# Making a 64-token tail as a 128-row chunk, and joining two batches' k-v products in one run, in an attention + bilinear FFN kernel on TensorE

## The chip, the cores and the metric

The kernel runs on one core of one Trainium2 chip. The metric is the device time of one execution in microseconds (us); the lower the better. A profile names the engines PE (TensorE matmuls), PEld (TensorE weight loads), DVE (VectorE), ACT (ScalarE), POOL (GpSimd) and SP (SyncE, whose queue issues many of the DMAs). In the code, `P` is the kernel's tile in PSUM, where its matmuls write; the second index of `P` is what is called a bank here. L258 is line 258 of the kernel that the profile belongs to, so a line that moved has another number after an edit: the attention chunk is L258 before and L265 after, the kv product is L168 in both.

## The reference, cut to what matters

```python
B, H, S, D = 8, 8, 576, 64           # batches, heads, tokens, head size
kv  = einsum('bhsd,bhse->bhde', k, v)        # per head 64 x 64
out = einsum('bhsd,bhde->bhse', q, kv)
x   = out / sqrt(mean(out**2, -1) + 1e-6) * g_norm    # per token and head
x   = x as (4608 tokens, 512)
y   = ((x @ w_a) * (x @ w_b)) @ w_out        # 512 -> 1536 -> 512
```

The last product chain is nearly all of the arithmetic. A batch has 576 tokens, which is four and a half times 128: each batch ends in a half chunk of 64 tokens.

## The kernel before

The FFN runs over nine strips of 512 tokens. A strip is 12 units `ffn_ab` (eight matmuls of 512 columns each) and 4 units `ffn_o` (twelve each). Strips 1 to 6 hold, between these dense units, the attention of the batch that the next strip needs: batch 2 in strip 1, and so on to batch 7 in strip 6. `slot(A, s, n)` is called after each unit with whole `n`, and in the middle of each with `n - 0.5`.

```python
# the product of k and v of one batch: 4 head pairs x 5 token chunks x 2 heads = 40 matmuls.
# Each has 64 weight columns; the two heads of a pair write rows 0 to 63 and rows 64 to 127 of o.
def kv(self, p, o):
    ...
    for c, n in enumerate(rows):
        for j in range(2):
            nc.tensor.matmul(o[j * D : (j + 1) * D, :],
                             lhsT=kk[0:n, 2 * p + j, c, :], rhs=vv[0:n, 2 * p + j, c, :], ...)

# one chunk of tokens of the batch: 4 matmuls, weights = q (tokens as columns)
def tx(self, c, i):
    t0 = c * 128
    n = min(128, S - t0)                    # the fifth chunk has n = 64
    for p in range(NP):
        nc.tensor.matmul(P[0:n, i, p * 128 : (p + 1) * 128],
                         lhsT=self.qT[:, p, t0 : t0 + n],
                         rhs=kvb[self.b % 2][:, p, :], start=True, stop=True)
    nc.scalar.activation(sqt[c % 3][0:n], P[0:n, i, :]..., AF.Square)
# then tss (DVE: sum), trs (ACT: 1/sqrt, POOL: times g), txt (DVE: product, SP: transpose to xt)

def slot(A, s, n):
    kb = P[:, 7, 0 : NP * D]...             # PSUM bank 7
    k0, xs = (5, (6.5, 8, 9.5, 11, 12.5)) if s == 1 else (2, (3.5, 5, 6, 7.5, 8.5))
    if n == k0:
        for p in range(NP):
            A.kv(p, kb[:, p, :])
        A.kv_out(slice(0, NP), kb)          # ACT copies kv to SBUF
    for c, x in enumerate(xs):
        i = 5 + c % 3                       # PSUM banks 5, 6, 7
        if n == x:         A.tx(c, i)
        elif n == x + 0.5: A.tss(c)
        elif n == x + 1:   A.trs(c)
        elif n == x + 2.5: A.txt(c, i)
# per strip: transpose q of batch b+1 at n = 8 (12 in strip 1), load batch b+2 at n = 14
```

## Time and profile before

The kernel takes 317.67 us (median of 3 runs, 317.66 to 318.12). Its profiled execution spans 316.0 us.

| before | value | view |
|---|---|---|
| PE busy | 309.6 us, 98% | engine table |
| DVE, ACT, POOL busy | 44%, 37%, 32% | engine table |
| chain that ended last, on PE | 95% | chain |
| PE's own waits | 2.9 us, all before 62 us | waits |
| a dense 512-column matmul, start to start | 215 to 217 ns | start times in the trace |

The engine table of before, and the chain of work that ended last, as shares of the span by engine and by line:

```profile
PE 309.6 (98%) x1907; PEld 147.0 (47%) x1907; DVE 138.5 (44%) x230; ACT 115.9 (37%) x229; POOL 101.7 (32%) x124
...
PE 95%; DMA 4%; issue 0%; POOL 0%; ACT 0%; POOLq 0%
PE P L312 59%; PE P L369 30%; PE P L258 2%; DMA qt<-in_q_dram 2%; DMA vt<-in_v_dram 2%; PE P L168 2%; PE P L219 0%; PE P L192 0%; PE P L245 0%; PE P L206 0%; ACT o_end L595 0%; POOL ident masks.py:199 0%; POOL ident masks.py:197 0%; POOLq masks.py:199 0%; POOLq L611 0%
```

The kernel is bound by PE. But "98% busy" does not say what PE loses: the record of a 512-column matmul lasts 379 ns while the next starts 216 ns later, so records overlap and paper over short pauses. What has to be read is the step from one start to the next. The waits of the weight loads give a first hint. Columns: who waited, for what, us in total, times, longest:

```profile
PEld L168 <- issue: 3.8, 10, 0.4
PEld L258 <- issue: 2.5, 6, 0.4
```

L258 runs 30 chunks, but only six of them show such a pause of 0.4 us: one a batch. Here are PE's instructions in order of time around a full chunk, around the last chunk of batch 5, and around its kv run. Columns: start in us, length, engine, line, operation, weight shape, matrix streamed, how many:

```profile
160.99 1.03 PE L312 MATMUL P<-xt,wb_t 128*128 128x512 bf16 x4
161.86 0.39 PE L258 MATMUL P<-kvb,qT 128*128 128x128 bf16 x4
162.08 1.03 PE L312 MATMUL P<-xt,wa_t 128*128 128x512 bf16 x4
...
167.71 1.03 PE L312 MATMUL P<-xt,wa_t 128*128 128x512 bf16 x4
168.66 0.41 PE L258 MATMUL P<-kvb,qT 128*64 128x128 bf16 x4
169.01 1.04 PE L312 MATMUL P<-xt,wb_t 128*128 128x512 bf16 x4
...
154.73 1.03 PE L312 MATMUL P<-xt,wb_t 128*128 128x512 bf16 x4
155.69 0.82 PE L168 MATMUL P<-vtl,ktl 128*64 128x64 bf16 x40
156.44 1.04 PE L312 MATMUL P<-xt,wa_t 128*128 128x512 bf16 x4
```

Four dense matmuls take 4 x 216 = 864 ns. So the full chunk adds 162.08 - 160.99 - 0.864 = 0.23 us, and the last chunk, with half the rows, adds 169.01 - 167.71 - 0.864 = 0.44 us. From the start times of single instructions (last dense start before to second dense start after, less two steps of 216) it is 224 ns against 447 ns, and 858 ns for a kv run. All figures of "what a piece adds" below are made in this way. The weight loads of the last chunk show where the pause sits:

```profile
167.71 0.53 PEld L312 LDWEIGHTS <-wa_t 128*128 128x128 bf16 x3
168.66 0.25 PEld L258 LDWEIGHTS <-qT 128*64 128x64 bf16 x4 [0.42 <-issue]
169.00 0.33 PEld L312 LDWEIGHTS <-wb_t 128*128 128x128 bf16 x3
```

The last dense matmul started at 168.354, and at the usual step of 216 ns the next matmul would have started at 168.57, but the next load of weights came only at 168.66, 308 ns after that start and 2 ns ahead of its own matmul. The first load of the full chunk at 161.86 us comes 214 ns ahead of its matmul, 3 ns after the start of the dense matmul before it.

### The profile page before, as it was taken

What the parts mean: (1) busy time and instruction counts of PE and PEld (TensorE: products, weight loads), DVE (VectorE), ACT (ScalarE), POOL (GpSimd) and SP (SyncE); (2) the same over time, 40 slices, a digit from 0 to 9 for tenths busy, and PEclk for the clock granted to TensorE, in tenths of its full rate; (3) what the DMA queues carried; (4) which work ended last, traced back from release to release, by engine and by line L of the source; (5) the groups of instructions that cost most, each with busy time, mean ns of one, the idle gap of its engine ahead of it and who ended that gap; (6) DMA issues with size and microseconds to landing.
All of it is one profiled execution on the core that took longest, in us unless ns stands there. A gap on an engine that the chain in (4) does not pass through costs nothing.

```text
span 316.0 us, 4979 instructions
## 1 busy us (share of the span) xinstructions
PE 309.6 (98%) x1907; PEld 147.0 (47%) x1907; DVE 138.5 (44%) x230; ACT 115.9 (37%) x229; POOL 101.7 (32%) x124
## 2 busy tenths in 40 slices
PE   7899999999999999999999999999999999999995
PEld 3444464444454444544454445444544444444443
DVE  4544335356337603771267224832475134213321
ACT  3643155453246214630455025512561232123310
POOL 8954890192543640346024801410041000000000
PEclk9999999999999999999999999999999999999999
DMA  8999999999999699069906992463012200030002
GB/s 177 197 196 199 200 183 156 228 126 172 173 172 136 119 173 184 17 127 133 227 10 125 133 229 21 81 104 100 2 35 72 105 0 0 33 97 5 0 35 100
DMA packets 94237, 36.19 MB, mean 115 GB/s; under 512 B 64902, under 2 KB 89734, under 8 KB 94214
## 3 DMA queue, kind: packets, MB, share of 16 engines
q0 software_dynamic: 59120, 18.44, 54.1%
q1 hardware_dynamic: 34738, 17.01, 23.8%
q10 hardware_dynamic: 356, 0.43, 0.4%
q8 instruction: 15, 0.25, 0.3%
q14 instruction: 8, 0.07, 0.1%
HBM read 37.78 MB, written 12.98 MB: 161 GB/s over the span
## 4 chain that ended last, share of the span: by engine, by line
PE 95%; DMA 4%; issue 0%; POOL 0%; ACT 0%; POOLq 0%
PE P L312 59%; PE P L369 30%; PE P L258 2%; DMA qt<-in_q_dram 2%; DMA vt<-in_v_dram 2%; PE P L168 2%; PE P L219 0%; PE P L192 0%; PE P L245 0%; PE P L206 0%; ACT o_end L595 0%; POOL ident masks.py:199 0%; POOL ident masks.py:197 0%; POOLq masks.py:199 0%; POOLq L611 0%
## 5 line engine op out<-in xcount | busy, mean ns | idle before, releaser
L330 DVE TENSOR_TENSOR ab<-P,asb 128x512 bf16<-128x512 f32 x108 | 74.5, 691 | 109.1 <-PE P L312 91.2
L312 PE MATMUL P<-xt,wa_t 128*128 128x512 bf16 x432 | 111.9, 379 | 0.0
L312 PE MATMUL P<-xt,wb_t 128*128 128x512 bf16 x432 | 111.8, 379 | 0.0
L326 ACT CAST asb<-P 128x512 bf16<-128x512 f32 x108 | 63.0, 585 | 90.9 <-PE P L312 90.9
L369 PE MATMUL P<-wo_t,ab 128*128 128x512 bf16 (+1 forms) x444 | 95.8, 374 | 0.0
L369 PEld LDWEIGHTS <-ab 128*128 128x128 bf16 x444 | 43.0, 98 | 48.7
L312 PEld LDWEIGHTS <-wb_t 128*128 128x128 bf16 x432 | 41.3, 98 | 47.7 <-DMA wb_t<-in_moe_w_b_dram 0.6
L312 PEld LDWEIGHTS <-wa_t 128*128 128x128 bf16 x432 | 41.1, 98 | 47.0 <-issue 0.2
L282 POOL TENSOR_TENSOR sqt<-rst,g_all 128x512 f32<-128x512 f32 (+1 forms) x24 | 25.0, 1044 | 98.7 <-ACT rst L275 98.7
L382 ACT COPY osb<-P 128x512 f32<-128x512 f32 x17 | 9.9, 585 | 71.9 <-PE P L369 67.3
L384 DVE COPY osb<-P 128x512 f32<-128x512 f32 x18 | 12.5, 692 | 46.5 <-PE P L369 32.9
L139 POOL DMA_DIRECT2D qs<-in_q_dram x12 | 19.8, 1653 | 1.2 <-issue 0.9
L271 DVE TENSOR_REDUCE sst<-sqt 128x8 f32<-128x512 f32 (+1 forms) x24 | 16.2, 677 | 2.0 <-ACT sqt L265 1.3
L292 DVE TENSOR_TENSOR qv<-P,sqt 128x512 bf16<-128x512 f32 (+1 forms) x24 | 16.3, 678 | 0.0
L265 ACT ACTIVATE sqt<-P 128x512 f32<-128x512 f32 (+1 forms) x24 | 14.3, 596 | 4.8 <-PE P L258 4.8
L258 PEld LDWEIGHTS <-qT 128*128 128x128 bf16 (+1 forms) x120 | 8.9, 100 | 8.2 <-issue 2.5
L258 PE MATMUL P<-kvb,qT 128*128 128x128 bf16 (+1 forms) x120 | 11.7, 220 | 0.0
L179 ACT CAST kvb<-P 64x256 bf16<-64x256 f32 (+1 forms) x20 | 6.0, 301 | 11.1 <-PE P L168 11.0
L233 DVE SCALAR_TENSOR_TENSOR xt<-P,g_col,rs 128x288 bf16<-128x288 f32 x16 | 7.5, 512 | 5.4 <-ACT rs L223 5.4
L275 ACT ACTIVATE rst<-sst,eps_t 128x8 f32<-128x8 f32 (+1 forms) x30 | 9.0, 301 | 2.0 <-DVE sst L271 2.0
L282 POOL TENSOR_TENSOR k_x<-rst,g_all 128x512 f32<-128x512 f32 x6 | 6.3, 1043 | 8.5 <-ACT rst L275 8.5
L131 POOL DMA_DIRECT2D wo_t<-in_moe_w_out_dram x12 | 6.4, 530 | 6.7 <-DMA wb_t<-in_moe_w_b_dram 3.3
(66 smaller groups left out, 119.4 us busy)
## 6 DMA issues: line engine op xcount, KB each, us to landing
out_dram<-osb SPq DMA_DIRECT2D x23, 256.0 KB, 2.3
qs<-in_q_dram POOLq DMA_DIRECT2D x12, 288.0 KB, 7.0
ktl<-in_k_dram POOLq DMA_DIRECT2D x6, 512.0 KB, 9.5
vtl<-in_v_dram POOLq DMA_DIRECT2D x6, 512.0 KB, 12.3
out_dram<-osb SPq DMA_DIRECT2D x13, 128.0 KB, 2.8
wo_t<-in_moe_w_out_dram POOLq DMA_DIRECT2D x12, 128.0 KB, 6.0
wa_t<-in_moe_w_a_dram POOLq DMA_DIRECT2D x5, 256.0 KB, 8.5
wb_t<-in_moe_w_b_dram POOLq DMA_DIRECT2D x5, 256.0 KB, 9.1
```

What stands on the lines that cost most here:

```text
L139: nc.gpsimd.dma_start(out=d[:, hs, :], in_=q[b, hs].rearrange("h t d -> t h d"))
L258: nc.tensor.matmul(P[0:n, i, p * 128 : (p + 1) * 128], lhsT=self.qT[:, p, t0 : t0 + n], rhs=kvb[self.b % 2][:, p, :], start=True, stop=True,)
L265: nc.scalar.activation(sqt[c % 3][0:n], P[0:n, i, :].rearrange("t (h d) -> t h d", h=H), AF.Square)
L271: nc.vector.reduce_sum(sst[c % 3][0:n], sqt[c % 3][0:n], axis=mybir.AxisListType.X)
L282: nc.gpsimd.tensor_mul(sqt[c % 3][0:n], rst[c % 3][0:n].unsqueeze(2).to_broadcast([n, H, D]), g_all[0:n].unsqueeze(1).to_broadcast([n, H, D]),
L292: nc.vector.tensor_mul(t[0:n], P[0:n, i, :].rearrange("t (h d) -> t h d", h=H), sqt[c % 3][0:n])
L312: nc.tensor.matmul(self.a if w is wa_t else self.b, lhsT=w[:, kc, self.fc * 128 : (self.fc + 1) * 128], rhs=xt[:, kc, t0 : t0 + STRIP], st ...
L326: nc.scalar.copy(self.t, self.a)
L330: nc.vector.tensor_mul(abt[self.s % 2][self.fc], self.b, self.t)
L369: nc.tensor.matmul(P[:, i, e0:e1], lhsT=abt[s % 2][fc][:, g * 128 : (g + 1) * 128], rhs=wo_t[:, fc, e0:e1], start=(fc == 0), stop=(fc == F ...
L382: nc.scalar.copy(t, P[:, i, :])
L384: nc.vector.tensor_copy(t, P[:, i, :])
```

## The change

Its intent: take pauses out of PE's stream. First, the fifth chunk of a batch is made with tokens 448 to 575, 128 rows; rows 0 to 63, which repeat tokens already done, are dropped. Second, kv of batches 4 and 5 is made in one run in strip 3, kv of 6 and 7 in one run in strip 5, so strips 4 and 6 have none. For that the k and v of batches 5 and 7 have to be there a strip earlier: q transposes and loads are called sooner, chunk places shift, and DVE copies the second batch's kv. The diff, cut to its core:

```diff
+        def rows(self, c):
+            t0 = min(c * 128, S - 128)
+            return t0, slice(c * 128 - t0, 128)
         def tx(self, c, i):
-            t0 = c * 128
-            n = min(128, S - t0)
+            t0, r = self.rows(c)
             for p in range(NP):
                 nc.tensor.matmul(
-                    P[0:n, i, p * 128 : (p + 1) * 128],
-                    lhsT=self.qT[:, p, t0 : t0 + n],
+                    P[:, i, p * 128 : (p + 1) * 128],
+                    lhsT=self.qT[:, p, t0 : t0 + 128],
   ...      (tss, trs, txt: rows 0:n become rows r, so the dropped half is not touched again)
     def slot(A, s, n):
-        k0, xs = (5, (6.5, 8, 9.5, 11, 12.5)) if s == 1 else (2, (3.5, 5, 6, 7.5, 8.5))
-        if n == k0:
-            for p in range(NP):
-                A.kv(p, kb[:, p, :])
-            A.kv_out(slice(0, NP), kb)
+        kb = P[:, 7, :].rearrange("q (b p e) -> q b p e", b=2, e=D)
+        if s == 1:
+            k0, xs = 5, (6.5, 8, 9.5, 11, 12.5)
+        else:
+            k0, x0 = {2: (2, 3.5), 3: (4, 5.5), 4: (0, 1.5), 5: (4, 5.5), 6: (0, 1.5)}[s]
+            xs = tuple(x0 + x for x in (0, 1.5, 2.5, 4, 5))
+        if n == k0 and s in (1, 2, 3, 5):
+            two = [A] if s < 3 else [A, Attn(s + 2)]
+            for i, a in enumerate(two):
+                for p in range(NP):
+                    a.kv(p, kb[:, i, p, :])
+            for i, a in enumerate(two):
+                a.kv_out(slice(0, NP), kb[:, i], nc.vector.tensor_copy if i else nc.scalar.copy)
   ...
-            if b + 1 < B and n == (12 if s == 1 else 8):
+            if b + 1 < B and n == (12, 4, 8, 5, 8)[s - 1]:
                 transpose_q(b + 1)
-            if b + 2 < B and n == 14:
+            if b + 2 < B and n == (14, 10, 14, 8)[s - 1]:
                 load_late(b + 2)
```

PE runs the same number of instructions before and after.

More of the change, by code (lines that the diff above doesn't have):

```diff
@@ L174, in kv, with kv_out @@
                     )
-        def kv_out(self, ps, src):
+        def kv_out(self, ps, src, copy=nc.scalar.copy):
             for j in range(2):
                 r = slice(j * D, (j + 1) * D)
-                nc.scalar.copy(kvb[self.b % 2][r, ps, r], src[r])
+                copy(kvb[self.b % 2][r, ps, r], src[r])
         def kv1(self, p, i):
@@ L251, in x, with by_head @@
                 )
+        def rows(self, c):
+            t0 = min(c * 128, S - 128)
+            return t0, slice(c * 128 - t0, 128)
+        def by_head(self, i):
+            return P[:, i, :].rearrange("t (h d) -> t h d", h=H)
         def tx(self, c, i):
-            t0 = c * 128
-            n = min(128, S - t0)
+            t0, r = self.rows(c)
             for p in range(NP):
                 nc.tensor.matmul(
-                    P[0:n, i, p * 128 : (p + 1) * 128],
-                    lhsT=self.qT[:, p, t0 : t0 + n],
+                    P[:, i, p * 128 : (p + 1) * 128],
+                    lhsT=self.qT[:, p, t0 : t0 + 128],
                     rhs=kvb[self.b % 2][:, p, :],
@@ L264, in tx, with tss, trs @@
                 )
-            nc.scalar.activation(
-                sqt[c % 3][0:n], P[0:n, i, :].rearrange("t (h d) -> t h d", h=H), AF.Square
-            )
-        def tss(self, c):
-            n = min(128, S - c * 128)
-            nc.vector.reduce_sum(sst[c % 3][0:n], sqt[c % 3][0:n], axis=mybir.AxisListType.X)
-        def trs(self, c):
-            n = min(128, S - c * 128)
-            nc.scalar.activation(
-                rst[c % 3][0:n],
-                sst[c % 3][0:n],
+            nc.scalar.activation(sqt[c % 3][r], self.by_head(i)[r], AF.Square)
+        def tss(self, c):
+            _, r = self.rows(c)
+            nc.vector.reduce_sum(sst[c % 3][r], sqt[c % 3][r], axis=mybir.AxisListType.X)
+        def trs(self, c):
+            _, r = self.rows(c)
+            n = r.stop - r.start
+            nc.scalar.activation(
+                rst[c % 3][r],
+                sst[c % 3][r],
                 AF.Abs_reciprocal_sqrt,
-                bias=eps_t[0:n],
+                bias=eps_t[r],
                 scale=1.0 / D,
@@ L282, in trs @@
             nc.gpsimd.tensor_mul(
-                sqt[c % 3][0:n],
-                rst[c % 3][0:n].unsqueeze(2).to_broadcast([n, H, D]),
-                g_all[0:n].unsqueeze(1).to_broadcast([n, H, D]),
+                sqt[c % 3][r],
+                rst[c % 3][r].unsqueeze(2).to_broadcast([n, H, D]),
+                g_all[r].unsqueeze(1).to_broadcast([n, H, D]),
             )
         def txt(self, c, i):
-            t0 = c * 128
-            n = min(128, S - t0)
+            t0, r = self.rows(c)
             t = x_tok[c // 3][:, c % 3]
-            nc.vector.tensor_mul(
-                t[0:n], P[0:n, i, :].rearrange("t (h d) -> t h d", h=H), sqt[c % 3][0:n]
-            )
+            nc.vector.tensor_mul(t[r], self.by_head(i)[r], sqt[c % 3][r])
             t0 += self.b * S
             nc.sync.dma_start_transpose(
-                xt[:, :, t0 : t0 + n], t[0:n].rearrange("t h d -> t (h d)")
+                xt[:, :, t0 + r.start : t0 + 128], t[r].rearrange("t h d -> t (h d)")
             )
@@ L547, in slot @@
     def slot(A, s, n):
-        kb = P[:, 7, 0 : NP * D].rearrange("q (p e) -> q p e", e=D)
-        k0, xs = (5, (6.5, 8, 9.5, 11, 12.5)) if s == 1 else (2, (3.5, 5, 6, 7.5, 8.5))
-        if n == k0:
-            for p in range(NP):
-                A.kv(p, kb[:, p, :])
-            A.kv_out(slice(0, NP), kb)
+        kb = P[:, 7, :].rearrange("q (b p e) -> q b p e", b=2, e=D)
[11 more added lines that the diff above has]
+                a.kv_out(slice(0, NP), kb[:, i], nc.vector.tensor_copy if i else nc.scalar.copy)
         for c, x in enumerate(xs):
```

## The prediction

> **What bounds the kernel now.** TensorE. In the engine table its matmuls are busy 309.6 of 316.0 us (98%); DVE 44%, ACT 37%, POOL 32%. In the chain that ended last PE holds 95%, 59% + 30% of it on the dense FFN lines (312 and 369). The waits view gives PE under 4 us of waits, all before 62 us. So an edit pays only what it takes out of PE's stream. In the strips PE's steps from start to start are regular: 215 to 217 ns for a dense 512-column matmul, granted clock full.
>
> **What the change removes, from PE start times in the trace.**
>
> 1. *The 64-row last chunk.* A full chunk of line 258 (four matmuls, 128x128 weights) starts 217 ns after the dense matmul before it, takes 56 ns per matmul, and the dense stream goes on without a pause: it adds 224 ns. The last chunk of each batch (128*64 weights, the same 128 columns streamed) starts 310 ns after the dense matmul, and the next dense matmul starts 152 ns after the chunk's last: it adds 447 ns. The excess of 224 ns is the same within 1 ns in all six batches. I read it as a change of array configuration from 128x128 to 128x64 and back. [...] With 128 rows no change of mode is left, and the dropped half costs nothing: what streams is 128 columns either way. Worth 6 x 0.224 = 1.34 us.
>
> 2. *Two kv runs less.* A kv run of line 168 (40 matmuls of 128x64, concurrent in pairs, 31.5 ns a pair) adds 858 ns, the same in all six. 20 pairs x 31.5 = 630 ns is work; 228 ns is entering and leaving the mode. Two of six runs merge into others: 2 x 0.228 = 0.46 us goes.
>
> Together 1.80 us, all on PE's chain.
>
> **What it adds and moves.** PE's instruction count stays. Two kv copies go from ACT to DVE (ACT's half copy takes 0.30 us; I estimate 0.35 to 0.4 on DVE from its 128x512 PSUM copy of 0.69), which is over half idle. Batches 5 and 7 are loaded sooner. I estimate from the trace that loads 5 start at about 106 us and land by 120 (7.0, 9.5, 12.3 us to landing for q, k, v), against kv at about 126; loads 7 from 167 to 180, against 192. Later chunks in strips 3 and 5 still finish before the next strip, which needs only the first ones. The q transposes are queued earlier on SP, but their sources have landed by then. Hence no new PE wait.
>
> **Predicted time:** 317.67 - 1.80 = 315.9 us; 8 in 10 between 315.4 and 316.6. Faster by over 2%: 0.01; within 2%: 0.98; slower by over 2%: 0.01.
>
> **What the profile would show.** Step 1: line 258's successor has one form only (128*128), last chunks add 224 ns like the others. Step 2: four kv runs, two of them of 80 matmuls adding about 1.49 us. Loads: no PE wait on DMA, ACT or DVE after 62 us. Span 316.0 to about 314.2.
>
> **What would make it wrong.** A k or v load landing late, with PE idle before a double kv run; a q transpose that waits for its load on the in-order SP queue and delays x transposes of the next strip; DVE held longer at its output copies by stores (13.5 us of such waits now); or an exit cost that grows with the merged run.

## The result, and the profile after

| | before | after |
|---|---|---|
| median, us | 317.69 (6 runs, 317.46 to 318.52) | 316.04 (6 runs, 315.68 to 316.41) |
| profiled span, us | 316.0 | 314.4 |
| PE, first kv run of strip 1 to PE's last start, us | 251.30 | 249.51 |
| PE before that first kv run, us | 61.03 | 61.27 |

The ratio is 0.9943 (95% interval 0.9929 to 0.9957). A ratio here is the mean time of one kernel's runs over that of the other's in the same rounds, so not quite the ratio of the medians quoted. Executions over 1.5% slower than the fastest of the same kernel are left out of the means. The clock granted was 0.998 to 1.0 of full speed.

The third row is the best measure of this change. The start-up, which the change does not touch, moves by up to 0.5 us from one profiled run to the next (60.79 to 61.27 us over all of them). PE's stretch from the first kv run to its last start repeats: three profiles of the changed kernel give 249.505, 249.504 and 249.505 us. It fell by 1.79 us.

The engine table and the chain after look as before, although the change worked; a gain of 0.6% does not show there:

```profile
PE 307.0 (98%) x1874; PEld 147.9 (47%) x1907; DVE 141.7 (45%) x234; ACT 115.8 (37%) x225; POOL 101.5 (32%) x124
...
PE 95%; DMA 1%; ACT 1%; issue 1%; DVE 0%; ACTq 0%
```

(33 matmul records are missing from this trace, 1874 of 1907; the busy time is short of them. Where a dense record is missing beside a piece, 216 ns are taken off what the piece seems to add.) The order of time around the last chunk of batch 4 and around the double kv run:

```profile
138.30 1.03 PE L315 MATMUL P<-xt,wa_t 128*128 128x512 bf16 x4
139.17 0.39 PE L265 MATMUL P<-kvb,qT 128*128 128x128 bf16 x4
139.39 1.03 PE L315 MATMUL P<-xt,wb_t 128*128 128x512 bf16 x4
...
124.69 1.03 PE L315 MATMUL P<-xt,wb_t 128*128 128x512 bf16 x4
125.65 1.46 PE L168 MATMUL P<-vtl,ktl 128*64 128x64 bf16 x80
127.04 1.04 PE L315 MATMUL P<-xt,wa_t 128*128 128x512 bf16 x3
```

The last chunk now adds 139.39 - 138.30 - 0.864 = 0.23 us like any other (223 ns from single starts), and the 80 matmuls add 1.49 us where two runs added 2 x 0.858 = 1.72. In the waits of the weight loads L265 has no entry left, and L168 has three fewer pauses: two are the two runs that are gone, the third lay in the start-up:

```profile
PEld L168 <- issue: 2.6, 7, 0.4
```

PE waits for no DMA, ACT or DVE after 62 us. DVE's copy of the second kv takes 422 ns, ACT's 366 ns; neither holds up PE. The groups of instructions by shape have these copies; the number before the second bar is the mean in ns. Before, ACT makes all of them:

```profile
L179 ACT CAST kvb<-P 64x256 bf16<-64x256 f32 x12 | 4.4, 366 | 6.3 <-PE P L168 6.2
```

After, DVE makes these four halves:

```profile
L179 DVE CAST kvb<-P 64x256 bf16<-64x256 f32 x4 | 1.7, 422 | 2.8 <-ACT kvb L179 2.8
```

### The profile page after: what moved, and what is told of

Its sections match the earlier page's. It is cut to its first block, busy times and chain, and to the rows that moved or that the text cites. A ratio compares the mean times of both kernels' runs of the same rounds, so it can differ in the third digit from the quotient of the medians.

```text
span 314.4 us, 4944 instructions
## 1 busy us (share of the span) xinstructions
PE 307.0 (98%) x1874; PEld 147.9 (47%) x1907; DVE 141.7 (45%) x234; ACT 115.8 (37%) x225; POOL 101.5 (32%) x124
## 4 chain that ended last, share of the span: by engine, by line
PE 95%; DMA 1%; ACT 1%; issue 1%; DVE 0%; ACTq 0%
PE P L315 59%; PE P L372 30%; PE P L265 2%; PE P L168 2%; DMA qv<-in_q_dram 1%; PE P L192 1%; PE P L219 1%; ACT asb L329 1%; PE P L400 1%; PE P L206 0%; ACT sq L215 0%; PE P L245 0%; DVE qc L447 0%; PE P L454 0%; ACT o_end L606 0%
## 5 line engine op out<-in xcount | busy, mean ns | idle before, releaser
L315 PE MATMUL P<-xt,wa_t 128*128 128x512 bf16 x420 | 110.7, 379 | 1.0 <-issue 0.2
L315 PE MATMUL P<-xt,wb_t 128*128 128x512 bf16 x423 | 109.7, 379 | 0.2
L265 PEld LDWEIGHTS <-qT 128*128 128x128 bf16 x120 | 9.2, 98 | 7.1
L265 PE MATMUL P<-kvb,qT 128*128 128x128 bf16 x120 | 11.6, 219 | 0.0
L179 ACT CAST kvb<-P 64x64 bf16<-64x64 f32 (+1 forms) x16 | 4.6, 285 | 10.4 <-PE P L168 10.3
```

The lines of the kernel that those rows point to most:

```text
L265: nc.tensor.matmul(P[:, i, p * 128 : (p + 1) * 128], lhsT=self.qT[:, p, t0 : t0 + 128], rhs=kvb[self.b % 2][:, p, :], start=True, stop=True,)
L315: nc.tensor.matmul(self.a if w is wa_t else self.b, lhsT=w[:, kc, self.fc * 128 : (self.fc + 1) * 128], rhs=xt[:, kc, t0 : t0 + STRIP], st ...
```

## The experiments

An array configuration is here the shape of a matmul's weights as the profile gives it, rows*columns: 128*128 or 128*64. The theory is that going from a 128x128 array configuration to 128x64 and back costs PE about 224 to 228 ns, whatever is done in between. Rivals: the chunk pays for its place or its waits; short weight loads are slow; the cost belongs to each matmul; the moved loads make part of the gain. "PE stretch" below is PE from the first kv run of strip 1 to its last start: 251.30 us before, 249.50 after. Eleven runs were made, all correct. Runs 5 and 6 are single looks, whose state is unknown; their granted clock was 1.0, and what is read from them are steps in the trace.

### 1 to 3. The parts of the change, one at a time

The first has the 128-row chunk alone.

```diff
 (the kernel before, with)
+ rows(), tx, tss, trs, txt of the changed kernel
```

> The kernel before with the 128-row last chunk alone; kv runs and loads as before. Theory (each 64-row chunk pays for two changes of array configuration): the last chunks add 224 ns to the dense stream instead of 447, six times, so PE from the first kv run of strip 1 to its last start takes 1.34 us less than the kernel before (249.96 against 251.30), and the time falls by about 1.3 us. Rival (the chunk's cost comes from its place at the end of the batch, that is from its waits, not its shape): the last chunks still add about 447 ns and nothing is gained.

Measured: 316.31 us, ratio 0.9955 (0.9943 to 0.9967); PE stretch 249.953 us, 1.346 less than before. All six last chunks add 223 ns. The rival of place and waits falls: the place is the same and the cost is gone.

The second has the double kv runs with all moves, and the 64-row chunk.

```diff
 (the changed kernel, with)
- rows(), tx, tss, trs, txt of the changed kernel
+ tx, tss, trs, txt of the kernel before
```

> The kernel before with the merged kv runs and the moved loads alone; the last chunk stays 64 rows. Theory (228 ns per run for entering and leaving): four kv runs, the double ones add about 1.49 us each, PE from the first kv run of strip 1 to its last start takes 0.46 us less than the kernel before. Rival (the overhead is per matmul, or grows with the run): the double runs add 2 x 858 = 1.72 us and nothing is gained.

Measured: 317.24 us, ratio 0.9984 (0.9971 to 0.9998); PE stretch 250.847, 0.452 less than before. The double runs add 1.49 us each. The cost is per run.

The third has the moves of loads, transposes and places, but no joined runs.

```diff
 (the kernel of the second, with)
-        if n == k0 and s in (1, 2, 3, 5):
-            two = [A] if s < 3 else [A, Attn(s + 2)]
+        if n == k0:
+            two = [A]
```

> The same moves of loads, q transposes and chunk places as in the merged kernel, but every batch keeps a kv run of its own, and the last chunk stays 64 rows. Theory: the moves are off PE's chain, so PE from the first kv run of strip 1 to its last start is the kernel before's 251.30 us within 0.05, and the time is the same within its noise. Rival (part of the gain comes from the moved loads): it is faster by up to 0.46 us.

Measured: 317.62 us, ratio 0.9996 (0.9983 to 1.0008); PE stretch 251.297 against 251.299. The moves by themselves give nothing. The parts add up: 1.346 + 0.452 = 1.798 us against 1.794 for the whole change.

### 4. The kv runs cut into pieces

```diff
 (the changed kernel, with)
+        for p in range(NP):
+            if s in (1, 2, 3, 5) and n == (k0 if s == 1 else k0 - 1.5 + 0.5 * p):
+                for i, a in enumerate(two):
+                    a.kv(p, kb[:, i, p, :])
         if n == k0 and s in (1, 2, 3, 5):
-            for i, a in enumerate(two):
-                for p in range(NP):
-                    a.kv(p, kb[:, i, p, :])
```

> The changed kernel with the kv runs of strips 2, 3 and 5 each cut into four pieces that lie half a unit of FFN work apart: 12 pieces instead of 3 runs, the same matmuls. Theory (about 228 ns for each entering and leaving): 9 x 0.228 = 2.05 us slower than the changed kernel, PE from the first kv run of strip 1 to its last start 251.55 instead of 249.50 us; each piece of a single kv adds about 0.386 us (5 pairs or 10 x 31.5 ns of work... 10 matmuls are 5 pairs, 158 ns, plus 228) and each piece of a double one about 0.543 us (10 pairs, 315 ns, plus 228). Rival (the cost belongs to the matmuls, or to a wait once per batch): no change within 0.1 us.

Measured: 318.98 us, ratio 1.0041 to the kernel before (1.0028 to 1.0055), so about 3 us slower than the changed kernel; PE stretch 252.455, which is 2.95 more and not 2.05. The pieces cost what was expected: 383 ns each in strip 2, 540 to 542 ns each in strips 3 and 5, but for one. Nine more entries and exits give 4 x 383 - 857 + 2 x (4 x 541 - 1491) = 2.02 us. The other 0.93 us are one event that I had not expected, in the first piece of strip 3:

```profile
122.30 1.03 PE L315 MATMUL P<-xt,wa_t 128*128 128x512 bf16 x4
123.26 0.35 PE L168 MATMUL P<-vtl,ktl 128*64 128x64 bf16 x10
124.02 0.67 PE L168 MATMUL P<-vtl,ktl 128*64 128x64 bf16 x10 [0.42 <-DMA vtl<-in_v_dram]
124.62 1.04 PE L315 MATMUL P<-xt,wb_t 128*128 128x512 bf16 x3
```

Batch 4's ten matmuls ran at once; batch 5's stood waiting for its v load. My edit starts that run at 123.26 us, the changed kernel at 125.65, and v was not there yet. So the rival falls (the cost is by entry, not by matmul), but one step of the prediction turns out badly measured: the margin of the moved loads is small. Run 7 looks at that.

### 5. The 64-row form inside a run

```diff
 (the kernel before, with, between A.kv and A.kv_out)
+            for p in range(NP):
+                nc.tensor.matmul(P[0 : S - 512, 7, 256:384],
+                    lhsT=A.qT[:, p, 512:S], rhs=kvb[A.b % 2][:, p, :], start=True, stop=True)
```

> The kernel before with four extra matmuls of the 64-row form (128x64 weights, 128 columns streamed, results unused) at the end of each of the six kv runs; the real last chunks stay as they are. Theory (the change of configuration costs, not the 64-row form): each kv run adds 858 + 4 x 56 = about 1080 ns, no more. Rival (the 64-row form is dear by itself, for instance because its weight loads take 106 to 113 ns instead of 98): each run adds 858 + 447 = about 1305 ns.

Measured, one look: 319.19 us; each run adds 1080 ns, which is 222 ns more than 858. One of these runs, with the extra four (L555):

```profile
122.97 0.82 PE L168 MATMUL P<-vtl,ktl 128*64 128x64 bf16 x40
123.63 0.39 PE L555 MATMUL P<-kvb,qT 128*64 128x128 bf16 x4
123.95 0.82 PE L312 MATMUL P<-xt,wa_t 128*128 128x512 bf16 x2
```

From the start of the run to the next dense matmul it is 0.98 us here and 0.75 in the run at 155.69 us of the kernel before. In the same trace the same four matmuls as a chunk of their own add 447 ns. The 64-row form is not dear; getting into it and out of it is.

### 6. The last chunk with 96 columns

```diff
 (the kernel before, q transposes in a tile with 64 spare columns qT_flat, with)
+            w = 128 if n == 128 else 96
-                    P[0:n, i, p * 128 : (p + 1) * 128],
-                    lhsT=self.qT[:, p, t0 : t0 + n],
+                    P[0:w, i, p * 128 : (p + 1) * 128],
+                    lhsT=qT_flat[self.b % 2][:, p * S + t0 : p * S + t0 + w],
```

> The kernel before with the last chunk made with 96 weight columns, the upper 32 rows dropped. Theory (a configuration of the array is what changes[...]): the last chunks add 224 ns, or little more. Rival 1 (any load of fewer than 128 weight columns is slow or cannot be pulled ahead): they add clearly more than 224 ns, with weight loads of 106 ns and over that start only after the dense matmul has streamed. Rival 2 (cost grows with what is missing from 128): about halfway, 335 ns.

Measured, one look: 316.51 us; PE stretch 249.954, the same as with 128 rows (249.953); the chunks add 223 ns. The groups of weight loads of the kernel before (count, then busy us and mean ns, then idle us before them and its cause):

```profile
L258 PEld LDWEIGHTS <-qT 128*128 128x128 bf16 x96 | 7.4, 98 | 5.7
L258 PEld LDWEIGHTS <-qT 128*64 128x64 bf16 x24 | 1.5, 109 | 2.5 <-issue 2.5
```

And with 96 columns:

```profile
L260 PEld LDWEIGHTS <-qT 128*128 128x128 bf16 x96 | 7.4, 98 | 5.7
L260 PEld LDWEIGHTS <-qT 128*96 128x96 bf16 x24 | 2.1, 123 | 1.3
```

The record of a load of 96 columns lasts 123 ns, longer than one of 64 columns (109) or of 128 (98), and yet the load costs nothing: the chunk adds 223 ns, and the idle time before these 24 loads is 1.3 us, none of it put down to a wait, where the loads of 64 columns have 2.5 us, all of it "issue". Nor is a record a step: in the 64-row chunk at 168.66 us the loads start 28 to 57 ns apart, while their records last 106 to 110 ns. So the length of a load's record is not what the last chunk paid for. Both rivals fall. That 96 columns would cost no change of configuration was an estimate of mine; the run shows that they cost none, not why.

### 7. The loads put back

```diff
 (the changed kernel, with)
-            if b + 1 < B and n == (12, 4, 8, 5, 8)[s - 1]:
+            if b + 1 < B and n == (12 if s == 1 else 8):
-            if b + 2 < B and n == (14, 10, 14, 8)[s - 1]:
+            if b + 2 < B and n == 14:
```

> The changed kernel with the q transposes and loads put back to where the kernel before has them in strips 2 and 4, kv runs still merged. In the cut kernel (e4) PE waited for the v load of batch 5 until about 123.9 us, so the margin of the changed kernel, whose double run starts at 125.65 us, is 2 to 2.5 us and not the 6 us of my prediction. The loads of batch 5 started at 107.9 us in the kernel before and at 106.5 in the changed one. Theory 1 (the moved loads only widen a margin): v lands near 125.5, PE waits less than 0.5 us, time within 0.1% of the changed kernel. Theory 2 (the moves are needed): PE waits over 1 us for v before the double run of strip 3.

Measured: 315.95 us, ratio 0.9948 (0.9935 to 0.9962), beside the changed kernel's 315.88 and 0.9945 (0.9931 to 0.9959) on the same chip, where one of its five runs, at 321.16 us, is left out of the ratio. PE stretch 249.518 against 249.504. The double runs add 1492 and 1504 ns against 1491. The last v transfer of batch 5 lands at 124.7 us (expected: 125.5), in time. So the earlier call of loads and transposes bought no time in these runs; it widens a margin. For batch 5 the margin widens little: its first load starts at 107.75 us here and at 106.31 in the changed kernel. There POOL, which issues the loads, is at work on the chunks before until about 106 us; here it waits another 1.55 us for the q transpose. For batch 7 the same wait is long:

```profile
174.49 0.18 POOL L136 COPY gate<-qT 1x1 bf16<-1x1 bf16 x1 [6.11 <-DMA qT<-qs]
174.73 3.31 POOL L139 DMA_DIRECT2D qs<-in_q_dram  x2
```

The changed kernel starts that load at 168.62 us. Here the last v transfer of batch 7 is issued at 180.48 us and lands 11.4 us later, at 191.90, and the first matmul that waits for it starts at 191.95. The margin was 0.05 us, and the landings of v in this run took from 9.6 to 12.5 us, so that PE did not stall was luck: the move of batch 7 is not idle, it keeps a load clear of PE's chain. (Whether the 13 ns that this double run adds come from it is not shown.)

### 8 and 9. A version that might beat both

Run 5 says that 64-row work is free of the change of configuration inside a kv run. There two matmuls can even run at once, as in kv, where the two heads' matmuls start 2 to 5 ns apart and a pair takes 31.5 ns. So the last 64 tokens of batches 2, 3 and 5, whose results are needed late enough, are moved to the kv run of the next strip.

```diff
 (the changed kernel, with, in strips 2, 3 and 5 between the kv products and kv_out, a function ptx)
+            for p in range(NP):
+                r = slice(p % 2 * D, (p % 2 + 1) * D)
+                nc.tensor.matmul(P[r, 6, p // 2 * 128 : (p // 2 + 1) * 128],
+                    lhsT=self.qT[:, p, S - 64 : S], rhs=kvb[self.b % 2][:, p, :],
+                    start=True, stop=True)
   ...      (sum, 1/sqrt, product on 128 rows x 4 heads; two transposes to xt; product at k0 + 2.5)
```

> A version that might beat both: the changed kernel, but the last 64 tokens of batches 2, 3 and 5 are made at the end of the kv run of the next strip, where the array already has the 128x64 configuration[...]. Theory (no change of configuration to pay for, and the two halves stream at the same time): each adds about 2 x 56 = 112 ns to its run instead of 223 as a chunk of its own; three of them make 0.33 us less on PE, from the first kv run to PE's last start 249.17 against 249.50 us, and the time 0.1% less. Rival (matmuls of 128 columns in the two halves do not overlap): each adds 224 ns and nothing is gained. Correctness must hold.

Measured: 315.99 us, ratio 0.9950 (0.9937 to 0.9964), no better than the changed kernel. Each packed chunk did add only 114 or 115 ns (972 - 857 and 1605 - 1491), about two steps of 56 ns for its four matmuls. But the PE stretch was 249.805, not 249.17. The loss is in three places like this one, in the second full chunk after the run:

```profile
93.98 1.03 PE L359 MATMUL P<-xt,wb_t 128*128 128x512 bf16 x4
95.05 0.38 PE L265 MATMUL P<-kvb,qT 128*128 128x128 bf16 x4
```

The chunk starts 428 ns after the last dense start instead of 216. It writes PSUM bank 6, which the packed chunk also uses, and whose last reader (the product on DVE) comes just half a unit before. 3 x 0.21 = 0.63 us, more than was won. The waits view blames "issue" for it, so the bank was an inference. The next run tests it by having that product half a unit earlier:

```diff
 (the kernel of run 8, with)
-            elif n == k0 + 2.5:
+            elif n == k0 + 2:
                 L.ptxt(6, 1)
```

> As e8, with the last reader of the packed chunk's PSUM bank half a unit earlier. In e8 each packed chunk added 114 ns to its run, as expected, but the second full chunk after it waited for its PSUM bank 212 ns longer than normal, three times: 0.63 us, which made PE 249.81 us instead of 249.17. Theory: with the bank free in time that wait is gone, and PE from the first kv run to its last start is 249.17 us, 0.33 less than in the changed kernel, the time 0.1% less. Rival (the wait is bound to the packed form, through the engines that finish it): 249.4 to 249.8 us again.

The same chunk of strip 2 in this run, in order of time:

```profile
94.02 1.03 PE L359 MATMUL P<-xt,wb_t 128*128 128x512 bf16 x4
94.89 0.39 PE L265 MATMUL P<-kvb,qT 128*128 128x128 bf16 x4
```

The pause is gone (0.87 us from unit to chunk again). PE stretch 249.177 us, 0.328 less than the changed kernel; time 315.37 us (315.29 to 315.49), ratio to before 0.9927 (0.9913 to 0.9940). The changed kernel beside it on the same chip:

> The changed kernel beside e9 on the same chip: PE from the first kv run of strip 1 to its last start 249.50 us within 0.03, 0.33 us more than e9; time 315.8 to 316.1 us.

It took 315.99 us (315.61 to 316.18), ratio 0.9944 (0.9932 to 0.9957), PE stretch 249.505. No run of one lies in the range of the other, though the two intervals of the ratios overlap. The medians differ by 0.62 us, more than the 0.33 that PE shows: in the profiles another 0.16 us lie behind PE's last start (3.45 against 3.61 us, and 3.46 in run 8), and 0.24 in the start-up, which varies anyway. Both packed kernels issue their last store 0.71 us after PE's last start, as the changed kernel does, so the 0.16 lie behind that store; why is open.

### The changed kernel once more

> The changed kernel itself once more, beside the two others on the same chip. Expected: 316.0 us, ratio 0.994 to 0.995 to the kernel before, PE from the first kv run of strip 1 to its last start 249.50 us within 0.03; the start of the first kv run may differ by 0.3 us from run to run.

Measured beside runs 7 and 8, as told there: 315.88 us, ratio 0.9945, PE stretch 249.504. The result repeats, and so does PE's part of it, to the nanosecond.

## Why the prediction was right

- **What bounds the kernel: right.** Every PE gain reached the time: 1.35 us of PE gave 1.41 us in the medians (run 1), 0.45 gave 0.48 (run 2), 0.00 gave 0.10 (run 3), each within the spread of the start-up.
- **Step 1, 1.34 us for six chunks: right.** Run 1 measured 1.346. That it is the change of configuration and not the 64-row form, the place or the speed of the weight load is shown by runs 1, 5 and 6. In the trace of the kernel before, the first weight load of each 64-row chunk starts 307 or 308 ns after the start of the last dense matmul, that of a full chunk 1 to 3 ns after it; the first dense load after a 64-row chunk starts 147 to 149 ns after the start of the chunk's last matmul, after a full chunk 1 to 3 ns. The pause is 94 ns going in (310 instead of 216) and 96 coming out (152 instead of 56); the other 34 of the 224 lie in the first step on either side (80 instead of 56, 226 instead of 216). What PE does in these pauses is not shown.
- **Step 2, 0.46 us for two runs: right.** Run 2 measured 0.452, and the double runs add 1.49 us as predicted. The feared exit cost that grows with the run does not show: runs of 10, 20, 40 and 80 matmuls add 383, 541, 858 and 1491 ns, which less 31.5 ns a pair leaves 226 to 231 ns for each.
- **No new PE wait: right in outcome, thinly.** The prediction let loads 5 "land by 120" with kv at about 126. Run 4 found v of batch 5 missing until about 124, and the first profile of the changed kernel has the same: the last v transfer of batch 5 lands at 124.26 us, and kv of batch 5, the second half of the double run of 125.65, needs it from about 126.4 (both from single records of the trace). So the margin is some 2 us, not 6. The mis-sized term is the landing. The durations of 7 to 12 us run from the issue of each transfer, not from the start of the group, and POOL reaches the v transfers last. POOL's issues of batch 5 in the changed kernel (start, length, what):

```profile
106.50 3.31 POOL L139 DMA_DIRECT2D qs<-in_q_dram  x2
109.79 0.92 POOL L142 DMA_DIRECT2D ktl<-in_k_dram  x1
110.69 0.71 POOL L146 DMA_DIRECT2D ktl<-in_k_dram  x1
111.36 0.92 POOL L142 DMA_DIRECT2D vtl<-in_v_dram  x1
112.23 0.73 POOL L146 DMA_DIRECT2D vtl<-in_v_dram  x1
```

How long these two v transfers took from issue to landing:

```profile
DMA to landing us min/median/max: 12.0/12.2/12.5
```

The last one is issued at 112.23; with its 12.0 us that is 124.2. In the same way loads 7 (last v issue at 174.7, 12.2 us) land at about 187 instead of "180", against kv at 191.5. SP's queue did stand still for a load in the changed kernel, 5.3 us for q of batch 4; its transpose started at 94.38 us and lasted 5.89, and the next x transpose started at 100.36. No PE wait came of it.
- **The kv copies: small misses.** ACT's was given as 0.30 us, which is the mean of a group that mixes two shapes; the 64x256 copy takes 0.366. DVE's, 0.35 to 0.4, takes 0.422. Neither is on PE's chain.
- **The time.** 317.67 - 1.80 = 315.9 against 316.04, 315.88 and 315.99 in three sets of runs. In the first profile PE's stretch gave 1.79 and the start-up took 0.24 back, by chance.

## What to carry to other kernels

On a kernel bound by TensorE, read start-to-start steps, not busy shares: each visit to 64 weight columns between matmuls of 128 cost 0.224 to 0.228 us here, and neither the busy share (98%) nor the chain (95%) showed it. Try padding a small matmul to the configuration of its neighbours if what it streams stays the same (six chunks gave 1.346 us here), or gathering what is narrow in one visit (two runs less gave 0.452); 96 columns were as good as 128 (223 ns a chunk). When work is pulled ahead of its loads, count the landing from the issue of the last transfer (12.0 us here), and after moving a chunk check who reads its PSUM bank last: a gain of 0.33 us was lost to three waits of 0.21.
